# Sigmoid attention and a skip mixture of experts: scores and values as four 64x64 float32 products side by side

## The chip, the cores and the metric

The kernel runs on one core of a Trainium2 chip. The time is the device time of one execution in microseconds (us); the time of a kernel is the median of its runs.

## The reference

First an attention over q, k, v of shape (batch 8, heads 12, sequence 448, head size 64), in which a sigmoid takes the place of the softmax, so no sum over keys is needed:

```python
scores = scale * np.matmul(q, k.transpose(0, 1, 3, 2)) - np.log(S)
attn = 1.0 / (1.0 + np.exp(-scores))
out = np.matmul(attn, v)
```

The heads of a token are joined to a row of 768 numbers, 3584 rows in all. Then a layer of 8 experts with a skip:

```python
do_compute = x @ w_skip > 0          # the other rows pass through
e_idx = argmax(x @ w_gate)           # one expert for each row
y = x + gate_w * (relu(x @ w1[e_idx]) @ w2[e_idx])
```

w1 is 768 x 1024 and w2 1024 x 768 for each expert. All is float32.

## The kernel before, in words

**Attention** is a loop over 48 steps, one for each batch `b` and pair of heads `hp`. The order of all instructions in it is written out by hand, so each engine works them off in the order of the program. A step does the following.

- `load` (L176) brings in k and q of the pair two steps ahead, each in four DMAs of 32 partitions from SyncE's (SP's) queue, and v in one DMA of 112 partitions. The 32-row pieces are laid so that a transpose of 32x32 blocks on VectorE (DVE) is enough to turn k and q: afterwards the 64 numbers of a head lie on 64 partitions, one head of the pair on the upper half of the partitions and the other on the lower.
- `prep` (L200) turns k and q with that transpose and splits each into a high part in the type float32r and the rest (on DVE, and for q on GpSimd, POOL).
- `scores` (L219) multiplies on TensorE (PE): for each of four chunks of 112 keys the three products high x high, high x rest and rest x high, for two heads side by side in the upper and the lower rows of the array. A product streams 448 columns (queries).
- `weigh` (L237) runs the sigmoid over a chunk of both heads on ScalarE (ACT), from PSUM to SBUF.
- `values` (L242) multiplies a chunk's weights by v in float32, two heads side by side in the left and the right columns of the array, each over 112 rows (keys), and sums four chunks in one PSUM tile `pa`. It works on the step before: while step n's scores are made, the values of step n-1 are summed. At the end of a step DVE copies `pa` into `xts`, the transposed rows of the batch.

Chunks go in pairs: scores of two chunks, sigmoid of both, values of two chunks of the step before. PSUM holds three tiles of one bank for transposes (`ps_t`), two of two banks for scores (`ps_s`) and one of one bank for values (`ps_a`).

**Beside attention**, in the steps of batch b the rows of batch b-1 are finished. After step hp 0 the `logits` of gate and skip are made (PE), after hp 1 `route` turns them and picks the expert (PE, DVE), in hp 2 `gates` and `route_count` give each token a place in its expert's list and POOL scatters the records. In hp 1 to 4 `rows` turns one quarter of the batch's rows back (three transposes for each half, on PE), ACT and DVE copy them out and ACT's queue writes them. A quarter holds every fourth token (`col`, L253). In step 3 a fill of the expert lists goes out on SP's queue. From step 35 (`W0`) on, the first expert's weights are loaded in 28 pieces on SP's queue and split by DVE and POOL (`wsplit`).

**The experts** follow: two blocks of the first expert, during whose products a plan of the other blocks is worked out, and then a loop over 128-row blocks, whose kinds (full, last of an expert, half, few rows) depend on the counts. Some of its small kinds multiply in plain float32 with two or four products side by side in columns of the array (L1271 and L1204).

Of the kernel before, what the change touches and what calls it, by code (L numbers as in the profile page):

```python
# [20 lines left out]
P = 128  # L21
# [3 lines left out]
def kernel(  # L25
# [18 lines left out]
    BT = 32  # L44
    NJ = S // BT
# [38 lines left out]
    nc.scalar.dma_start(wcat[:, :, 0:NE], w_gate.rearrange("(k p) e -> p k e", p=P))  # L84
    with nc.allow_non_contiguous_dma(reason="one small vector"):
        nc.scalar.dma_start(
            wcat[:, :, NE : NE + 1], w_skip.rearrange("(k p o) -> p k o", p=P, o=1)
        )
# [13 lines left out]
    nc.gpsimd.iota(tok_i, pattern=[[1, NC]], base=0, channel_multiplier=NC)  # L102
# [45 lines left out]
        tc.tile_pool(name="ps_t", bufs=3, space=bass.MemoryType.PSUM)  # L148
# [23 lines left out]

    warm = const.tile([P, 1], F32, name="warm")
    nc.scalar.activation(warm, bias, AF.Sigmoid)

    def load(b, hp, q_eng=nc.sync):  # L176

        t = []  # L180
        n = (NJ - 1) * D + BT
        for nm, src, eng in (("k", k, nc.sync), ("q", q, q_eng)):
            x = io.tile([P, NJ * D], F32, tag=nm, name=f"{nm}_{b}_{hp}", bufs=2)
            for h in range(2):
                for i in range(ND):
                    p = h * D + i * BT
                    eng.dma_start(
                        x[p : p + BT, :n],
                        src[b, 2 * hp + h].rearrange("(r j) d -> r (j d)", j=NJ)[:, i * BT : i * BT + n],
                    )  # L190
            t.append(x)
        x = io.tile([CP, 2, NC, D], F32, tag="v", name=f"v_{b}_{hp}", bufs=3)
        nc.sync.dma_start(
            x.rearrange("p h c d -> p h (c d)"),
            v[b, 2 * hp : 2 * hp + 2].rearrange("h (p c) d -> p h (c d)", c=NC),
        )
        t.append(x)
        return t

    def prep(b, hp, kt, qt, first=False):  # L200

        out = []
        xs = wk.tile([P, 2, S], F32, tag="b0", name=f"x_{b}_{hp}")
        for nm, t, low in (("k", kt, nc.vector), ("q", qt, nc.gpsimd)):
            x = xs[:, len(out)]
            nc.vector.transpose(  # L206
                x.rearrange("p (r j) -> p j r", j=NJ),
                t.rearrange("p (j d) -> p j d", d=D)[:, :, :BT],
            )
            hl = wk.tile([P, 2, S], F32R, tag=nm + nm, name=f"{nm}{nm}_{b}_{hp}")  # L210
            if first:
                nc.scalar.activation(hl[:, 0], x, AF.Copy)  # L212
            else:
                nc.vector.tensor_copy(hl[:, 0], x)  # L214
            (nc.vector if first else low).tensor_tensor(hl[:, 1], x, hl[:, 0], op=ALU.subtract)  # L215
            out.append(hl)
        return out

    def scores(b, hp, cs, kk, qq):  # L219
        sc = {  # L220
            c: ps_s.tile([P, 2, 512], F32, tag="s", name=f"s_{b}_{hp}_{c}") for c in cs
        }
        for c in cs:

            for n, (a, w) in enumerate(((0, 0), (0, 1), (1, 0))):
                for j in range(2):
                    r = slice(j * D, (j + 1) * D)
                    nc.tensor.matmul(  # L228
                        sc[c][:CP, j, :S],
                        kk[r, a, c::NC],  # L230
                        qq[r, w, :],
                        start=(n == 0),
                        stop=(n == 2),
                    )
        return [sc[c] for c in cs]
# [1148 lines left out]
```

## Time and profile before

| | |
|---|---|
| median of 3 runs | 665.95 us (665.94 to 670.04) |
| profiled execution | 661.53 us |
| its span, first to last instruction | 659.8 us |
| mean granted clock of TensorE | 0.975 |
| busy PE / PE weight loads / DVE / ACT / POOL | 610.8 / 407.0 / 384.7 / 285.6 / 232.0 us |
| moved by DMA | 119.78 MB, mean 182 GB/s |

The profile is one execution. PE is TensorE's products, PEld its weight loads, which may overlap products, DVE VectorE, ACT ScalarE, POOL GpSimd, SP SyncE; an engine's name with a q is its queue of DMA issues. A group line gives line of the kernel, engine, operation, what is written and read, partitions x elements, the count after an x, then busy us, mean ns of one, and the idle time of the engine before them with what ended it. A float32 product of PE stands as two records. A timeline line begins with start and length in us; neighbouring instructions of one kind are merged, and the ends of products are modelled, so the lines of PE overlap a little: what counts is the distance from start to start. A line of the windows gives a stretch, its length, and for each engine busy us and instructions, then PE's granted clock, the DMA engines' busy share and GB/s. A line of the chain with a start and a length gives the time a group held the chain of work that ended last.

### The profile page before, as it was taken

The numbers are of one execution on the slowest core, as the hardware profiler recorded it, in microseconds if no ns is written. First come the engines' busy times: TensorE is split into PE (matmuls) and PEld (weight loads), VectorE is DVE, ScalarE is ACT, GpSimd is POOL, SyncE is SP. The second block draws the span as 40 slices with busy tenths as digits, with TensorE's granted clock in tenths as the row PEclk, the third lists the DMA queues.
The fourth block names the chain that finished last, engine by engine and source line by source line (L and its number), as shares of the span: only waits on it lengthen the run. The fifth ranks groups of instructions, "written<-read, shape, count | busy, mean of one in ns | idle before, by whom it ended". The sixth has DMA issues, their size and how long they took to land.

```text
span 659.8 us, 13758 instructions
## 1 busy us (share of the span) xinstructions
PE 610.8 (93%) x3843; PEld 407.0 (62%) x3844; DVE 384.7 (58%) x839; ACT 285.6 (43%) x463; POOL 232.0 (35%) x328
## 2 busy tenths in 40 slices
PE   5999999999999999998998999979799999999592
PEld 4555655656556555554454488968576768678382
DVE  4645766757667558588778466135733343437941
ACT  3654555555555546554454432226423212236430
POOL 1112411311313213156546632223822433437740
PEclk7999999999999999999999999998899999999797
DMA  9686665575775566696896413480484857869100
GB/s 187 174 252 170 177 182 167 181 208 148 207 209 171 152 187 187 193 247 191 242 231 201 143 43 99 116 323 3 136 292 154 309 193 243 289 231 338 41 20 25
DMA packets 62322, 119.78 MB, mean 182 GB/s; under 512 B 14036, under 2 KB 28132, under 8 KB 62272
## 3 DMA queue, kind: packets, MB, share of 16 engines
q1 hardware_dynamic: 52112, 99.01, 50.4%
q10 hardware_dynamic: 6128, 11.50, 5.8%
q0 software_dynamic: 4032, 8.65, 4.1%
q8 instruction: 25, 0.41, 0.3%
q14 instruction: 25, 0.20, 0.1%
HBM read 111.07 MB, written 17.86 MB: 195 GB/s over the span
## 4 chain that ended last, share of the span: by engine, by line
PE 75%; issue 7%; DMA 7%; DVE 4%; POOL 3%; ACT 1%; SPq 1%; ACTq 0%; POOLq 0%; DVEq 0%
PE pa L244 19%; PE s L228 18%; PE ph L509 9%; PE py L536 8%; PE px L283 4%; PE b_ph L509 3%; PE b_py L536 3%; DMA k<-in_k_dram 2%; PE ph L1271 2%; DMA q<-in_q_dram 2%; PE py L1271 2%; PE pxt L485 2%; PE pl L265 1%; PE ph L1204 1%; DMA lst<-fill 1%
## 5 line engine op out<-in xcount | busy, mean ns | idle before, releaser
L238 ACT ACTIVATE at<-s,bias 112x896 f32<-112x896 f32 x192 | 183.2, 1004 | 133.3 <-PE s L228 130.5
L228 PE MATMUL s<-qq,kk 64*112 64x448 f32 x1152 | 157.8, 405 | 11.5 <-ACT qq L212 5.1
L244 PE MATMUL pa<-at,v 112*64 112x448 f32 x752 | 165.6, 554 | 3.1 <-DVE xt L664 2.0
L228 PEld LDWEIGHTS s<-qq,kk 64*112 64x112 f32 x1152 | 127.2, 281 | 54.4 <-ACT at L238 23.6
L215 POOL TENSOR_TENSOR qq<-x,qq 128x448 fp32r<-128x448 f32 x47 | 53.8, 1144 | 220.9 <-DVE qq L214 159.4
L244 PEld LDWEIGHTS pa<-at,v 112*64 112x64 f32 x752 | 44.6, 135 | 60.3 <-issue 52.6
L206 DVE STREAM_TRANSPOSE x<-k 128x448 f32<-128x448 f32 x48 | 46.1, 960 | 16.9 <-DMA k<-in_k_dram 16.2
L283 PEld LDWEIGHTS px<-ident,xt 128*112 128x112 f32 x192 | 25.2, 188 | 40.2 <-issue 39.5
L664 DVE COPY xt<-pa 128x448 f32<-128x448 f32 x47 | 29.1, 620 | 35.4 <-PE pa L244 35.4
L292 DVE COPY xr<-px 112x384 f32<-112x384 f32 x28 | 15.6, 556 | 56.0 <-PE px L283 56.0
L206 DVE STREAM_TRANSPOSE x<-q 128x448 f32<-128x448 f32 x48 | 46.1, 961 | 2.3 <-DMA q<-in_q_dram 2.2
L414 POOL DMA_INDIRECT lst<-rec,idx x32 | 32.3, 1009 | 26.3 <-DVE xr L292 16.1
L283 PE MATMUL px<-ident,xt 128*112 128x128 f32 x192 | 36.4, 302 | 0.5 <-ACT xr L290 0.5
L518 ACT ACTIVATE hs<-ph 128x512 f32<-128x512 f32 x16 | 9.6, 600 | 62.6 <-PE ph L509 62.6
L479 POOL TENSOR_TENSOR wl<-wr,wh 128x384 fp32r<-128x384 f32 (+1 forms) x28 | 32.4, 1182 | 11.0 <-DVE wh L478 10.3
L509 PE MATMUL ph<-wh,xh 128*128 128x512 f32 x96 | 29.5, 409 | 5.0 <-issue 4.6
L536 PE MATMUL py<-wh,hh 128*128 128x384 f32 x128 | 33.8, 345 | 0.0
L536 PE MATMUL py<-wh,hl 128*128 128x384 f32 x128 | 32.7, 336 | 1.0 <-DVE hl L529 1.0
L529 DVE TENSOR_TENSOR hl<-pht,hh 128x512 fp32r<-128x512 f32 x16 | 11.0, 690 | 38.3 <-ACT hh L528 36.3
L215 DVE TENSOR_TENSOR kk<-x,kk 128x448 fp32r<-128x448 f32 x48 | 32.0, 666 | 1.6
L536 PE MATMUL py<-wl,hh 128*128 128x384 f32 x128 | 32.6, 335 | 0.0
L509 PE MATMUL ph<-wl,xh 128*128 128x512 f32 x96 | 30.4, 408 | 0.0
(276 smaller groups left out, 841.5 us busy)
## 6 DMA issues: line engine op xcount, KB each, us to landing
raw<-in_moe_w_dram SPq DMA_DIRECT2D x84, 256.0 KB
raw<-in_moe_w_dram SPq DMA_DIRECT2D x56, 384.0 KB
k<-in_k_dram SPq DMA_DIRECT2D x192, 108.0 KB
q<-in_q_dram SPq DMA_DIRECT2D x188, 108.0 KB
v<-in_v_dram SPq DMA_DIRECT2D x48, 224.0 KB
out_dram<-xr ACTq DMA_DIRECT2D x32, 336.0 KB
wr<-in_moe_w_dram SPq DMA_DIRECT2D x12, 256.0 KB
wr<-in_moe_w_dram SPq DMA_DIRECT2D x16, 192.0 KB
```

The costliest lines, as they stand in the source:

```text
L206: nc.vector.transpose(x.rearrange("p (r j) -> p j r", j=NJ), t.rearrange("p (j d) -> p j d", d=D)[:, :, :BT],)
L215: (nc.vector if first else low).tensor_tensor(hl[:, 1], x, hl[:, 0], op=ALU.subtract)
L228: nc.tensor.matmul(sc[c][:CP, j, :S], kk[r, a, c::NC], qq[r, w, :], start=(n == 0), stop=(n == 2),)
L238: nc.scalar.activation(at[c], sc[:CP, :, :S], AF.Sigmoid, bias=bias[:CP], scale=SCALE)
L244: nc.tensor.matmul(pa[j * D : (j + 1) * D, :S], vt[:, j, c, :], at[c][:, j, :], start=(c == 0), stop=(c == NC - 1),)
L283: nc.tensor.transpose(px[:CP, j * P : (j + 1) * P], xt[:, 3 * h + j, col(c)], ident,)
L414: put = nc.gpsimd.indirect_dma_start(out=lst[:, :], out_offset=bass.IndirectOffsetOnAxis(ap=idx[:, c : c + 1], axis=0), in_=rec[:, c, :], ...
L479: nc.gpsimd.tensor_tensor(lo, r, hi, op=ALU.subtract)
L509: nc.tensor.matmul(ph[h], a[:, j * P : (j + 1) * P], w[j][h], start=(n == 0), stop=(n == len(t) - 1),)
L536: nc.tensor.matmul(py[:, o, :H2], a[h][:, js], w[j][:, o * H2 : (o + 1) * H2], start=(j == 0 and n == 0), stop=(j == NK2 - 1 and n == 2),)
L664: nc.vector.tensor_copy(xts[prev[0]][:, prev[1], :], pa[:, :S])
L1271: nc.tensor.matmul(dst[g * MD : (g + 1) * MD, :n], a, w, start=(j == 0), stop=(j == most - 1), tile_position=(0, g * MD),)
```

## The change

- **Scores** are one float32 product for each head and chunk, without split. The 448 keys are taken as seven groups of 64 (every seventh key). A chunk `c` below 3 holds two of the groups (c and 4 + c); for each of two heads and two key groups there is one 64x64 product of 448 columns, the heads in the upper and lower rows of the array, the key groups in its left and right columns. Chunk 3 holds the seventh group (3): its two column halves take half of the queries each, 224 columns.
- **Values** use the same four parts: rows by key group, columns by head. The two row halves sum into two banks of `pa`, and DVE adds these: a copy of the first bank and an addition of the second (`add_values`).
- The values come **two chunks behind** the scores, in one line that runs across the steps, instead of a step behind.
- k and q are **loaded for two steps** by the same four DMAs of 32 partitions each, now with two runs in a row; v for two steps by two DMAs of 64 partitions with four of seven key groups each. Two buffers of each. The first step's k and q are loaded alone, q from ACT's queue ahead of the gate weights, which came first before.
- One chunk gives the place for the other work: after the scores of chunk 2, `rows` turns both halves at once, and logits and their turning stand there too (in the steps of hp 0 and 1), ahead of the values of that place. Row quarters hold 112 neighbouring tokens.
- PSUM: two tiles for transposes, two for scores of two banks, one for values of two banks. Some tiles of the experts' first blocks move to other buffers.

```diff
     ps_t = ctx.enter_context(
-        tc.tile_pool(name="ps_t", bufs=3, space=bass.MemoryType.PSUM)
+        tc.tile_pool(name="ps_t", bufs=2, space=bass.MemoryType.PSUM)
     )
...
+    def load_kq(b, hp, n, k_eng=nc.sync, q_eng=nc.sync, part=None, t=None):
+        if t is None:
+            t = [
+                wk.tile([P, n, NJ * D], F32, tag=nm, name=f"{nm}_{b}_{hp}", bufs=2) for nm in "kq"
+            ]
+        m = (NJ - 1) * D + BT
+        gs = slice(0, n) if part is None else slice(part, part + 1)
+        for x, src, eng in zip(t, (k, q), (k_eng, q_eng)):
             for h in range(2):
                 for i in range(ND):
                     p = h * D + i * BT
+                    a = src[b, 2 * hp : 2 * (hp + n)].rearrange(
+                        "(g h) (r j) d -> h r g (j d)", h=2, j=NJ
                     )
+                    eng.dma_start(x[p : p + BT, gs, :m], a[h, :, gs, i * BT : i * BT + m])
         return t
+    def load_v(b, hp, n):
+        x = io.tile([P, 2 * n, NV, D], F32, tag="v", name=f"v_{b}_{hp}", bufs=2)
+        a = v[b, 2 * hp : 2 * (hp + n)]
+        for m in range(2):
+            nc.sync.dma_start(
+                x[m * D : (m + 1) * D].rearrange("p h c d -> p h (c d)"),
+                a.rearrange("h (p c) d -> p h (c d)", c=NR7)[:, :, 3 * m * D : (3 * m + NV) * D],
+            )
+        return x
...
+    def scores(b, hp, c, xs):
+        sc = ps_s.tile([P, 2, 512], F32, tag="s", name=f"s_{b}_{hp}_{c}")
+        for m in range(2):
+            first, qs = (4 * m + c, slice(0, S)) if c < 3 else (3, slice(m * HQ, (m + 1) * HQ))
+            for j in range(2):
+                r = slice(j * D, (j + 1) * D)
+                nc.tensor.matmul(
+                    sc[m * D : (m + 1) * D, j, : qs.stop - qs.start],
+                    xs[r, 0, first::NR7],
+                    xs[r, 1, qs],
+                    start=True,
+                    stop=True,
+                )
+        return sc
...
+    def values(pa, c, vt, at):
+        for r in range(2):
+            rs = slice(r * D, (r + 1) * D)
+            qs = slice(0, S) if c < 3 else slice(r * HQ, (r + 1) * HQ)
+            for j in range(2):
+                nc.tensor.matmul(
+                    pa[j * D : (j + 1) * D, r, qs],
+                    vt[rs, j, r + c if c < 3 else 3 * (1 - r), :],
+                    at[rs, j, : qs.stop - qs.start],
+                    start=(c == 0),
+                    stop=(c == 3),
+                )
+    def add_values(b, hp, pa):
+        nc.vector.tensor_copy(xts[b][:, hp, :], pa[:, 0, :S])
+        nc.vector.tensor_tensor(xts[b][:, hp, :], xts[b][:, hp, :], pa[:, 1, :S], op=ALU.add)
...
+        if n % 2 and n + 3 < N:
+            kq[(n + 3) // 2] = load_kq(*steps[n + 3], 2)
...
+        for c in range(4):
+            at = wk.tile([P, 2, S], F32, tag="A", name=f"at_{b}_{hp}_{c}", bufs=5)
+            sc = scores(b, hp, c, xs)
+            weigh(c, sc, at)
+            if c == 0 and nxt:
+                xs_next = prep(*nxt, part(n + 1)[0])
+            if c == 2:
+                if hp == 0 and b > 0:
+                    pl = ps_t.tile([P, 512], F32, tag="t", name=f"pl_{pb}")
+                    logits(pl, range(NK1), xts[pb], 2)
+                if hp == 1 and b > 0:
+                    lg = turn_logits(pb, lts[pb])
+                rc = hp - (1 if b == B - 1 else 2)
+                if 0 <= rc < NC and b > 0:
+                    xr = new_xr(pb, rc)
+                    for h in range(2):
+                        rows(pb, rc, h, xts[pb], xr)
+            if len(line) == 2:
+                next_values()
+            line.append((b, hp, c, vt, at))
+            if c == 1:
+                if nxt:
+                    prep(*nxt, part(n + 1)[1], xs_next)
+                if n % 2 == 0 and n + 2 < N:
+                    vs[n // 2 + 1] = load_v(*steps[n + 2], 2)
...
```

`next_values` takes the oldest chunk of `line`, calls `values` for it and, after chunk 3, `add_values`; `prep` is one transpose for k (chunk 0) and one for q (chunk 1).

More of the change, by code (lines that the diff above doesn't have):

```diff
@@ L44 @@
     BT = 32
+    NR7 = S // D
+    NV = (NR7 + 1) // 2
     NJ = S // BT
@@ L83 @@
     nc.vector.memset(wcat, 0.0)
[L84 to L88, printed above, removed]
     ones = const.tile([CP, P], BF16, name="ones")
@@ L197, in load @@
[L197 to L217, printed above, removed]
@@ new lines, in prep @@
+    def prep(b, hp, t, xs=None):
+        n = 0 if xs is None else 1
+        if xs is None:
+            xs = wk.tile([P, 2, S], F32, tag="b0", name=f"x_{b}_{hp}")
+        nc.vector.transpose(
+            xs[:, n].rearrange("p (r j) -> p j r", j=NJ),
+            t.rearrange("p (j d) -> p j d", d=D)[:, :, :BT],
+        )
+        return xs
+    def scores(b, hp, c, xs):
[12 more added lines that the diff above has]
+        return sc
@@ L578, with part @@
     order.__enter__()
-    ld = {n: load(*steps[n], nc.scalar if n == 0 else nc.sync) for n in range(2)}
+    kq = {0: load_kq(0, 0, 2, nc.sync, nc.scalar, 0)}
+    load_kq(0, 0, 2, part=1, t=kq[0])
+    nc.scalar.dma_start(wcat[:, :, 0:NE], w_gate.rearrange("(k p) e -> p k e", p=P))
+    with nc.allow_non_contiguous_dma(reason="one small vector"):
+        nc.scalar.dma_start(
+            wcat[:, :, NE : NE + 1], w_skip.rearrange("(k p o) -> p k o", p=P, o=1)
+        )
+    warm = const.tile([P, 1], F32, name="warm")
+    nc.scalar.activation(warm, bias, AF.Sigmoid)
+    vs = {0: load_v(0, 0, 2)}
+    kq[1] = load_kq(*steps[2], 2)
+    def part(n):
+        return [t[:, n % 2] for t in kq[n // 2]]
     idle = ps_s.tile([P, 2, 512], F32, tag="s", name="idle")
@@ L585, in keep_busy, with next_values @@
             nc.tensor.matmul(idle[:, 0, :P], ident, ident, start=True, stop=True)
-    keep_busy(5)
-    pr = {0: prep(*steps[0], ld[0][0], ld[0][1], True)}
-    pr[1] = prep(*steps[1], ld[1][0], ld[1][1])
-    keep_busy(5)
-    prev = None
+    keep_busy(10)
+    xs = prep(*steps[0], part(0)[0])
+    xs = prep(*steps[0], part(0)[1], xs)
     xts, lts, rts = {}, {}, {}
     wrs = []
-    xr = None
+    line = []
+    pa = None
+    def next_values():
+        nonlocal pa
+        b, hp, c, vt, at = line.pop(0)
+        if c == 0:
+            pa = ps_a.tile([P, 2, 512], F32, tag="a", name=f"pa_{b}_{hp}")
+        values(pa, c, vt, at)
+        if c == 3:
+            add_values(b, hp, pa)
     for n, (b, hp) in enumerate(steps):
@@ L667 @@
         wrs = wrs_next
-        prev = (b, hp, ld.pop(n)[2], at)
-        if b > 0 and hp == 0:
-            pl = ps_t.tile([P, 512], F32, tag="t", name=f"pl_{pb}")
-            logits(pl, range(NK1), xts[pb], 2)
-            lts[pb] = keep_logits(pb, pl)
-        if b > 0 and hp == 1:
-            rts[pb] = route(pb, lts[pb])
+        xs = xs_next
     lb = B - 1
@@ L718 @@
     logits(pl, range(NK1 - 1), xt, 4)
-    pa = ps_a.tile([P, 512], F32, tag="a", name="pa_last")
-    for c in range(NC):
-        values(pa, c, prev[2], prev[3])
-    nc.vector.tensor_copy(xt[:, NPAIR - 1, :], pa[:, :S])
+    for _ in range(2):
+        next_values()
+    px = ps_s.tile([P, 2, 512], F32, tag="s", name="b0_px")
     for h in range(2):
-        px = ps_t.tile([P, 512], F32, tag="t", name=f"b0_px{h}")
-        turn_x(x0[0], h, px)
-        split_x(h, px, xh0, xl0)
+        turn_x(x0[0], h, px[:, h])
+        split_x(h, px[:, h], xh0, xl0)
     logits(pl, [NK1 - 1], xt, 4)
@@ L1015 @@
         gemm2(j, hh0, hl0, py)
-    pxt = [
-        ps_a.tile([P, 512], F32, tag="a", name="pxt0"),
-        ps_t.tile([P, 512], F32, tag="t", name="pxt1"),
-    ]
+    pxt2 = ps_a.tile([P, 2, 512], F32, tag="a", name="pxt")
+    pxt = [pxt2[:, h, :] for h in range(2)]
     for h in range(2):
```

127 lines of the change are left out of this document (36 added, 91 removed).

## The prediction, made before the changed kernel ran

> **What bounds the kernel now.** I read the page's parts 1 to 4 first, then its groups, then the timeline of TensorE alone (PE), because the question is how long one attention step occupies it.
>
> ```profile
> span 659.8 us, 13758 instructions
> PE 610.8 (93%) x3843; PEld 407.0 (62%) x3844; DVE 384.7 (58%) x839; ACT 285.6 (43%) x463; POOL 232.0 (35%) x328
> PE 75%; issue 7%; DMA 7%; DVE 4%; POOL 3%; ACT 1%; SPq 1%; ACTq 0%; POOLq 0%; DVEq 0%
> ...
> L238 ACT ACTIVATE at<-s,bias 112x896 f32<-112x896 f32 x192 | 183.2, 1004 | 133.3 <-PE s L228 130.5
> L228 PE MATMUL s<-qq,kk 64*112 64x448 f32 x1152 | 157.8, 405 | 11.5 <-ACT qq L212 5.1
> L244 PE MATMUL pa<-at,v 112*64 112x448 f32 x752 | 165.6, 554 | 3.1 <-DVE xt L664 2.0
> ```
>
> PE holds 75% of the chain that ended last, and scores (L228) and values (L244) are its two costliest groups. ACT, which turns scores into weights (L238), waited 130.5 us for scores, so it is not the limit. A step that carries only attention, and the start of a batch's extra work, look like this:
>
> ```profile
> 272.12 1.61 PE L228 MATMUL s<-qq,kk 64*112 64x448 f32 x12
> 273.65 1.72 PE L244 MATMUL pa<-at,v 112*64 112x448 f32 x8
> 275.31 1.60 PE L228 MATMUL s<-qq,kk 64*112 64x448 f32 x12
> ...
> 238.19 1.60 PE L228 MATMUL s<-qq,kk 64*112 64x448 f32 x12
> ...
> 282.97 1.60 PE L228 MATMUL s<-qq,kk 64*112 64x448 f32 x12
> ```
>
> From 272.12 to 275.31 passes half a step: two score chunks in 1.53 and two value chunks in 1.66, 3.19 in all, so **6.37 us a step**. The last two rows follow the logits of consecutive batches, so a batch of six steps takes 44.78. Less 6 x 6.37, **6.56 us** are left for the batch's other PE work (logits, row turning, counting). PE has no gaps here: attention is bound by PE.
>
> I cut the span at four marks:
>
> ```profile
> 50.02 0.57 PE L228 MATMUL s<-qq,kk 64*112 64x448 f32 x2 [1.28 <-DVE qq L214]
> 268.94 1.60 PE L228 MATMUL s<-qq,kk 64*112 64x448 f32 x12
> 374.77 1.20 PE L265 MATMUL pl_last<-xt,wcat 128*32 128x448 f32 x16
> ```
>
> Steps 0 to 5 end at 50.0; steps 6 to 34 take 218.9; steps 35 to 47, beside which the first expert's weights are loaded, take 105.8; the experts take the last 285.0. By PE work alone the third stretch would take 13 x 6.37 + 2 x 6.56 = 95.9, so about 10 us of it are stalls.
>
> **The new step on PE.** Which width a product streams at is seen in the expert code, where float32 products already run side by side in column parts of the array:
>
> ```profile
> 478.25 5.31 PE py L1271 x32
> 532.62 2.73 PE ph L1204 x48
> ```
>
> L1271 has two products of 384 columns side by side, 8 groups: 5.31 / 8 = 0.664. L1204 has four of 256 columns, 6 groups: 2.73 / 6 = 0.455. Read as one line, these give 1.63 ns a column and 0.037 us a group; two or four at once seems to make no difference. A group of 448 columns is then 0.768 us, one of 224 columns 0.402.
>
> The change has, per step, three score groups of 448 columns and one of 224, and the same for values: 6 x 0.768 + 2 x 0.402 = **5.41 us a step**, 0.96 less than 6.37. Today's values take 4 x 0.83 and would take 2.71; scores go from 3.05 to 2.71. The lower bound has no cost per group: 7 x 448 x 1.63 ns = 5.11. The upper bound gives every group the start that today's value block pays when PE turns from scores to values, 1.66 - 2 x 0.73 = 0.20: 5.11 + 8 x 0.20 = 6.7. I take the line through the two rows, since they show products of the same type, run after run in one shape, as the new groups would be. The assumption is that the parts may lie side by side in rows and columns at once; no row of before shows that for float32. Rows side by side are seen for scores only:
>
> ```profile
> 308.55 0.28 PEld L228 LDWEIGHTS s<-qq,kk 64*112 64x112 f32 x2 [0.70 <-issue]
> 329.74 1.32 PEld L228 LDWEIGHTS s<-qq,kk 64*112 64x112 f32 x12 [0.70 <-ACT at L238]
> 60.21 0.20 PEld L244 LDWEIGHTS pa<-at,v 112*64 112x64 f32 x4 [0.21 <-issue]
> 60.21 1.72 PE L244 MATMUL pa<-at,v 112*64 112x448 f32 x8
> 60.64 0.14 PEld L244 LDWEIGHTS pa<-at,v 112*64 112x64 f32 x2 [0.23 <-issue]
> 61.02 0.14 PEld L244 LDWEIGHTS pa<-at,v 112*64 112x64 f32 x2 [0.23 <-issue]
> ```
>
> Twelve score weight loads fill 1.32 of the 1.53 us, about 0.1 each, one after another: today's scores go at the pace of their weight loads. In the new step a group has eight loads of 64 columns. At 0.1 each they would be 0.8 a group, as long as the group; but the value rows show four such loads in 0.20 and the rest inside the products, and 64 columns are fewer than 112. I cost them at nothing beyond the 0.037; uncovered, they are the slower rival below.
>
> The Trainium skill, "TensorE: Matmul & The Clock Gate", section "The mechanism" of Part 3, says that a weight load overlaps products in flight only where its row group differs; two of the four new parts always share one. By that rule the 0.14 us loads would lie bare twice a group. This trace disagrees: the value loads at 60.64 and 61.02 share all rows with the products that run from 60.21 on, and the block still takes 1.66.
>
> **What hangs on the step.** ACT has three sigmoid passes of 896 elements and one of 448: 3 x 1.00 + an estimated 0.5 (half of it) = 3.5 us, below 5.41; the products that need them are two chunks away, about 3 us after the pass begins, so they hide. DVE loses the float32r splits and gains a second pass on the values:
>
> ```profile
> L664 DVE COPY xt<-pa 128x448 f32<-128x448 f32 x47 | 29.1, 620 | 35.4 <-PE pa L244 35.4
> L215 DVE TENSOR_TENSOR kk<-x,kk 128x448 fp32r<-128x448 f32 x48 | 32.0, 666 | 1.6
> L206 DVE STREAM_TRANSPOSE x<-k 128x448 f32<-128x448 f32 x48 | 46.1, 960 | 16.9 <-DMA k<-in_k_dram 16.2
> L215 POOL TENSOR_TENSOR qq<-x,qq 128x448 fp32r<-128x448 f32 x47 | 53.8, 1144 | 220.9 <-DVE qq L214 159.4
> ...
> 40.64 1.72 PE L244 MATMUL pa<-at,v 112*64 112x448 f32 x8
> 42.41 0.62 DVE L664 COPY xt<-pa 128x448 f32<-128x448 f32 x1 [2.48 <-PE pa L244]
> ```
>
> Two turns, a copy and an add (sized like the subtraction, 0.67) are 0.96 x 2 + 0.62 + 0.67 = 3.2 us a step, beside PE. POOL loses 1.14. The added wait: there is one values accumulator, so the next step's first value group waits for copy and add. The value block begun at 40.64 gives way after 1.66, at 42.30, and its copy starts 0.1 later; with as much for the way back that is 0.1 + 0.62 + 0.67 + 0.1 = 1.49 us, and PE has only one score group (0.77) to do meanwhile, with everything behind it in PE's order held: **0.7 us** bare. In batches 1 to 7 the logits or row turning stand at that place (6.56 / 6 is about 1.1 a step) and hide it; in steps 1 to 5 and 47 nothing does: 6 x 0.7 = 4.2.
>
> **Loads.** The same bytes of k and q (8 x 108 KB a step), values 256 KB instead of 224, in issues for two steps.
>
> ```profile
> k<-in_k_dram SPq DMA_DIRECT2D x192, 108.0 KB
> v<-in_v_dram SPq DMA_DIRECT2D x48, 224.0 KB
> out_dram<-xr ACTq DMA_DIRECT2D x32, 336.0 KB
> wr<-in_moe_w_dram SPq DMA_DIRECT2D x12, 256.0 KB
> wr<-in_moe_w_dram SPq DMA_DIRECT2D x16, 192.0 KB
> ...
> core 0: us, PE busy (x) PEld busy (x) DVE busy (x) ACT busy (x) POOL busy (x), PEclk, DMA share, GB/s
> 232.00:277.00 45.00, 44.78 (x296) 26.23 (x296) 30.79 (x70) 25.30 (x30) 11.02 (x12) 1.00 0.64 184
> 277.00:290.00 13.00, 13.00 (x88) 6.75 (x88) 9.22 (x16) 7.51 (x9) 5.68 (x5) 1.00 0.92 245
> 290.00:330.00 40.00, 35.78 (x216) 19.37 (x214) 33.47 (x61) 18.54 (x22) 23.70 (x22) 1.00 0.77 222
> ```
>
> A batch moves 6 x 1120 + 4 x 336 KB = 8.26 MB. A new batch on PE is 6 x 5.41 + 6.56 = 39.0 us: 212 GB/s, against 245 / 0.92 = 266 at full engines. The loads of k and q come out of SP's queue as soon as the second turn of the step before frees the tile, more than two steps (over 12 us) ahead; a pair needs 2240 KB, 8.6 us at 266. So they hide. In steps 35 to 44 they don't: 5 x 1728 (k, q) + 4 x 512 (v) + 4800 (21 weight pieces) + 6 x 336 (rows out) = 17.5 thousand KB, 17.9 MB, 67 us at 266, against 10 x 5.41 + about 10.5 = 65 on PE. There **DMA is late next**; with about 3 us of mismatch 70, and 19 for the last three steps: 89 instead of 105.8.
>
> **Start and end.**
>
> ```profile
> 6.85 0.95 DVE L206 STREAM_TRANSPOSE x<-k 128x448 f32<-128x448 f32 x1 [5.29 <-DMA k<-in_k_dram]
> 9.49 0.94 DVE L206 STREAM_TRANSPOSE x<-q 128x448 f32<-128x448 f32 x1 [0.43 <-DMA q<-in_q_dram]
> 11.09 5.20 PE L228 MATMUL s<-qq,kk 64*112 64x448 f32 x24 [5.13 <-ACT qq L212]
> ```
>
> Today q's issues stand behind the small gate loads and the table load on ACT. With those behind q, k and q should land together near 6.9; two turns later, at 8.8, scores start, without the 1.6 us of splitting: 2.3 earlier (bounds 0 and 4). Steps 0 to 5: 8.8 + 6 x 5.41 + 5 x 0.7 + about 1.7 (an estimate for the first values' load) = 46.5 instead of 50.0. At the end two value groups instead of four chunks remain: about 1.7 less, 283.3; the smaller transpose pool (two buffers for three) could take that back, 0 to +4.
>
> **Sum.** 46.5 + (29 x 5.41 + 5 x 6.56 + 0.7 = 190.4) + 89 + 283.3 = 609.2 us of span, against 659.8: -51. The profiled execution took 661.5 in all, the median of the runs is 665.95; I subtract from the median: **615 us**.
>
> **Rivals.** (1) Loads bind more: at the 222 GB/s that 290 to 330 reached while PE idled 4.2 of 40 us, the 17.9 MB take 81 instead of 70, and the pairs come late once or twice elsewhere: 11 + 4 more, 630. For it: stretch three stalls today; against: the batches need only 212. Chance 0.14. (2) Each group pays a start of 0.12 to 0.20, because the chunks alternate between two accumulators and wait on other engines: 6.07 to 6.7 a step, 0.66 to 1.29 more than forecast; the 35 steps up to the last stretch and the 3 after its loads feel it in full and the ten between mostly: 645 to 675. For it: that is what today's blocks pay; against: shape no longer changes between them. 0.09. (3) Slower: weight loads of the parts that share rows lie bare, 0.14 twice a group: 5.11 + 16 x 0.14 = 7.35 a step, 0.98 over today's, x 48 = 47 less 5 at start and end: 708. It decides from 0.08 bare per load on, where the step is 6.37 again. For it: scores today show loads in a line; against: the value block. 0.06. The cited rule of the Trainium skill speaks for this one. (4) The change does not do what it says: the parts run two and two, 10.8 a step, 4.4 x 48 more than today: about 870. 0.03.
>
> **How the numbers follow.** The forecast has 0.68. Its own range: no cost per group (0.3 a step, -9 in steps 6 to 34), loads without mismatch and start at its best (-3 each) give 600; the end's +4, the start's +2 and 0.04 more a group (0.3 a step, +9) give 630. To hold 8 in 10 the range takes rival 1 and the near end of rival 2: **600 to 643**. Within 1% (about what a measurement of this kernel can tell from no change) lies part of rival 2: 0.04. Slower by over 1% are rivals 3 and 4 and the far end of 2: 0.09. Faster 0.87.
>
> **What would show it.** Plain steps of 5.4 us from score group to score group, with groups 0.77 long; six waits of PE for the add, 0.7 each, in steps 1 to 5 and 47; a first score near 8.8; DMA share over 0.9 and waits for k in steps 35 to 44; an unchanged loop over experts. I am wrong if the groups take over 0.85, if DVE waits for k in the middle batches, or if the add takes over 1 us.

## The result, and the profile after

The changed kernel took **639.94 us** (median of 4 executions, 637.68 to 644.19) against 666.33 for the kernel before on the same chip: a ratio of 0.960, 95% interval 0.955 to 0.965. A second measurement beside other variants gave 641.84 (638.44 to 646.49), ratio 0.964 (0.957 to 0.972). The forecast was 615 with a range of 600 to 643: direction and range hold, but of the forecast gain only half came. The time lies 3 us inside the range, in the room that the range left for rivals; the forecast's own range, 600 to 630, was missed.

The page of the changed kernel's profiled execution (the one of 644.19 us), its engines and the groups of scores (L220) and values (L241):

```profile
PE 573.6 (90%) x4995; PEld 376.1 (59%) x4996; DVE 332.2 (52%) x744; ACT 276.1 (43%) x461; POOL 175.7 (28%) x281
...
L241 PE MATMUL pa<-at,v 64*64 64x448 f32 (+1 forms) x1536 | 170.4, 506 | 19.2 <-DVE xt L251 17.8
L220 PE MATMUL s<-x 64*64 64x448 f32 (+1 forms) x1536 | 170.1, 506 | 5.4 <-DVE x L205 4.7
```

TensorE is busy 37 us less. Waits for the addition of the two value banks (L251), 17.8 us, are new. Where the span went, by the marks of the prediction; in each profile step 6 and step 35 begin with the first scores line of that step (48.98 and 236.72 in the first profile, 49.26 and 237.36 in the second):

| stretch, us | before | forecast | after | second profile of after |
|---|---|---|---|---|
| steps 0 to 5 | 50.0 | 46.5 | 49.0 | 49.3 |
| steps 6 to 34 | 218.9 | 190.4 | 187.7 | 188.1 |
| steps 35 to 47, to the last logits | 105.8 | 89 | 104.7 | 106.9 |
| from there to the end | 285.0 | 283.3 | 296.4 | 287.3 |
| span | 659.8 | 609.2 | 637.8 | 631.6 |
| time less span | 1.7 | taken as unchanged | 6.4 | 7.3 |

The whole gain lies in steps 6 to 34. The last 13 steps, for which 17 us were forecast, gave nothing.

The timeline of TensorE in a step of the first batch (start, length, then what was done; a row ends with the idle time before it and its releaser):

```profile
30.34 0.96 PE L220 MATMUL s<-x 64*64 64x448 f32 x8
31.09 0.96 PE L241 MATMUL pa<-at,v 64*64 64x448 f32 x8
...
32.59 0.59 PE L241 MATMUL pa<-at,v 64*64 64x224 f32 x8
32.97 0.96 PE L220 MATMUL s<-x 64*64 64x448 f32 x8
34.66 0.98 PE L241 MATMUL pa<-at,v 64*64 64x448 f32 x8 [0.73 <-DVE xt L251]
...
91.01 1.34 PE L266 MATMUL pl<-xt,wcat 128*32 128x448 f32 x16
129.76 1.34 PE L266 MATMUL pl<-xt,wcat 128*32 128x448 f32 x16
246.45 1.34 PE L266 MATMUL pl<-xt,wcat 128*32 128x448 f32 x16
300.85 1.34 PE L266 MATMUL pl<-xt,wcat 128*32 128x448 f32 x16
341.42 1.15 PE L266 MATMUL pl_last<-xt,wcat 128*32 128x448 f32 x16
```

A group of four products comes every 0.75 us at 448 columns and every 0.38 at 224 (forecast 0.768 and 0.402), so a step holds 5.25 us of attention. The row at 34.66 is the bare wait for copy and add. The logits rows lie one batch of six steps apart: 38.75 between the first two (all five early batches: 38.5 to 39.2, forecast 39.0), then **54.40 for steps 36 to 41** and 40.57 for steps 42 to 47.

What stands in the 54.40 is seen in five views of the same profile: TensorE, then VectorE ahead of the longest wait, then VectorE's waits from 246 to 341 us (total, times, longest), then three of the waits of SP's queue in the same stretch, then the issues of that queue.

```profile
257.85 1.77 PE L241 MATMUL pa<-at,v 64*64 64x448 f32 x8 [4.05 <-DVE xt L251]
292.54 1.77 PE L241 MATMUL pa<-at,v 64*64 64x448 f32 x8 [6.40 <-DVE xt L251]
...
288.04 0.43 DVE L482 CAST wh<-wr 128x512 fp32r<-128x512 f32 x1 [7.08 <-DMA wr<-in_moe_w_dram]
...
290.35 0.93 DVE L205 STREAM_TRANSPOSE x<-k 128x448 f32<-128x448 f32 x1
291.14 0.59 DVE L250 COPY xt<-pa 128x448 f32<-128x448 f32 x1
291.77 0.62 DVE L251 TENSOR_TENSOR xt<-xt,pa 128x448 f32<-128x448 f32 x1
...
DVE wh L482 <- DMA wr<-in_moe_w_dram: 18.8, 9, 7.1
...
SPq L473 <- DMA out_dram<-xr: 9.4, 2, 7.2
SPq L186 <- DMA out_dram<-xr: 9.2, 2, 5.7
SPq L194 <- DMA out_dram<-xr: 8.6, 2, 5.4
...
240.46 9.19 SPq L186 DMA_DIRECT2D q<-in_q_dram  x4
250.73 2.52 SPq L473 DMA_DIRECT2D wr<-in_moe_w_dram  x5
```

VectorE stands 7.08 us at a cast (L482) whose weight piece has not landed. The turn of k, the copy and the add of the next step are behind it in VectorE's order; the add ends at 292.4, and TensorE goes on at 292.54. Before, all such waits for pieces were 0.7 us in sum. In a step SP asks for the pieces behind k and q, and the four q issues that begin at 240.46 and stand ahead of pieces took 9.19 us. SP's waits name what held the queue longest: from 246 to 341 us issues of pieces (L473), of k and q (L186) and of v (L194) stood 27.2 us until a row store (`out_dram<-xr`, rows written out from ScalarE's queue) had landed. Such holds alone do no harm: the four q issues at 226.47 took 9.15 us, and TensorE lost nothing by it. No run took the row stores away, so how much of the loss they make is open.

### The profile page after: what moved, and what is told of

Same layout as the page of the kernel before. It is cut to its first block, busy times and chain, and to the rows that moved or that the text cites. A ratio compares the mean times of both kernels' runs of the same rounds, so it can differ in the third digit from the quotient of the medians.

```text
span 637.8 us, 15511 instructions
## 1 busy us (share of the span) xinstructions
PE 573.6 (90%) x4995; PEld 376.1 (59%) x4996; DVE 332.2 (52%) x744; ACT 276.1 (43%) x461; POOL 175.7 (28%) x281
## 5 line engine op out<-in xcount | busy, mean ns | idle before, releaser
L233 ACT ACTIVATE at<-s,bias 128x896 f32<-128x896 f32 x192 | 175.2, 914 | 134.7 <-PE s L220 127.0
L241 PE MATMUL pa<-at,v 64*64 64x448 f32 (+1 forms) x1536 | 170.4, 506 | 19.2 <-DVE xt L251 17.8
L220 PE MATMUL s<-x 64*64 64x448 f32 (+1 forms) x1536 | 170.1, 506 | 5.4 <-DVE x L205 4.7
L220 PEld LDWEIGHTS s<-x 64*64 64x64 f32 x1536 | 82.8, 191 | 63.0 <-issue 39.1
L241 PEld LDWEIGHTS pa<-at,v 64*64 64x64 f32 x1536 | 59.9, 136 | 71.5 <-issue 56.0
L205 DVE STREAM_TRANSPOSE x<-k 128x448 f32<-128x448 f32 x48 | 45.9, 957 | 24.5 <-DMA k<-in_k_dram 13.6
L284 PEld LDWEIGHTS px<-ident,xt 128*112 128x112 f32 x192 | 20.1, 133 | 20.2 <-issue 17.5
L251 DVE TENSOR_TENSOR xt<-xt,pa 128x448 f32<-128x448 f32 x48 | 29.8, 620 | 1.6
L499 DVE TENSOR_TENSOR xl<-pxt,xh 128x384 fp32r<-128x384 f32 x30 | 16.4, 554 | 26.5 <-ACT xh L495 26.1
L284 PE MATMUL px<-ident,xt 128*112 128x128 f32 x192 | 28.0, 280 | 1.7 <-ACT xr L291 1.7
L540 PEld LDWEIGHTS py<-wh,hl 128*128 128x128 f32 x128 | 24.2, 197 | 8.5 <-DVE hl L533 8.5
```

Of the source, the lines that this page charges most:

```text
L205: nc.vector.transpose(xs[:, n].rearrange("p (r j) -> p j r", j=NJ), t.rearrange("p (j d) -> p j d", d=D)[:, :, :BT],)
L220: nc.tensor.matmul(sc[m * D : (m + 1) * D, j, : qs.stop - qs.start], xs[r, 0, first::NR7], xs[r, 1, qs], start=True, stop=True,)
L233: nc.scalar.activation(at[:, :, :n], sc[:, :, :n], AF.Sigmoid, bias=bias, scale=SCALE)
L241: nc.tensor.matmul(pa[j * D : (j + 1) * D, r, qs], vt[rs, j, r + c if c < 3 else 3 * (1 - r), :], at[rs, j, : qs.stop - qs.start], start=( ...
L251: nc.vector.tensor_tensor(xts[b][:, hp, :], xts[b][:, hp, :], pa[:, 1, :S], op=ALU.add)
L284: nc.tensor.transpose(px[:CP, j * P : (j + 1) * P], xt[:, 3 * h + j, col(c)], ident,)
```

## The experiments

The question of most of them is why steps 35 to 47 gained nothing. The reading above, theory A of the first one: the first expert's weight pieces come late, VectorE stands at their casts, and TensorE waits for the add behind them. Each expectation says what its own letters mean. "Steps 36 to 41" and "42 to 47" are the distances between logits rows; the changed kernel has 54.4 and 40.6 there (54.3 and 42.8 in its second profile).

**No weight transfers.** Each cast reads one small tile filled once, in place of a piece that was loaded.

```diff
-        nc.sync.dma_start(r, src[ds(ev, 1), ...])
+        r = wz[:, :n]
```

> The changed kernel without the 28 transfers of the first expert's weights: their casts and subtractions stay, but read one constant tile, so the first expert's result is left out. Theory A (in steps 35 to 47 the casts on DVE stand in its order ahead of the turns and the add, and wait for weight pieces that land late; PE then waits for the add): the four long PE waits of 4.1, 1.2, 6.4 and 2.1 us go, steps 36 to 41 take 39 to 40 us like the batches before, not 54.4, and the time falls by 14 to 18 us to about 624. Theory B (the stretch is set by something on PE or ACT, such as a lower granted clock): steps 36 to 41 stay above 48 us, time 636 to 642.

621.4 us, span 616.9 (one execution). Steps 36 to 41 took 39.9, steps 42 to 47 37.8; no wait of TensorE over 1 us is left in them. Logits rows and TensorE, VectorE and DMA from 246 to 300 us (the columns are length, busy us and instructions of the five engines, granted clock, DMA share, GB/s):

```profile
250.84 1.34 PE L266 MATMUL pl<-xt,wcat 128*32 128x448 f32 x16
290.71 1.34 PE L266 MATMUL pl<-xt,wcat 128*32 128x448 f32 x16
...
246.00:300.00 54.00, 52.37 (x597) 28.20 (x594) 39.05 (x77) 31.39 (x39) 25.62 (x25) 1.00 0.87 201
```

So all that the last stretch lost hangs on these 6.3 MB of transfers: 77.7 us against 95.0 for the twelve steps.

**The pieces asked for ahead of k and q** in SP's queue, the rest unaltered.

```diff
+        if 0 <= n - W0 < len(how_many):
+            for _ in range(how_many[n - W0]):
+                wrs_next.append(wload(units.pop(0), ev0))
         if n % 2 and n + 3 < N:
             kq[(n + 3) // 2] = load_kq(*steps[n + 3], 2)
...
-        if 0 <= n - W0 < len(how_many):
-            for _ in range(how_many[n - W0]):
-                wrs_next.append(wload(units.pop(0), ev0))
```

> The changed kernel with one move: in each step the weight pieces are issued on SP's queue ahead of the k and q loads of that step, not behind them. The bytes are the same. Theory A (the pieces are late because they are issued late, behind 1.7 MB of k and q that have over two steps of time): DVE's waits for pieces, 18.8 us, fall below 6 and the time falls by 8 to 13 us, to 627 to 632. Theory B (the DMA engines are full in this stretch, whatever the order): the waits move to k and q, the time stays within 3 us of 640.

629.36 us (627.88 to 634.44), ratio to the kernel before 0.941 (0.937 to 0.946), as theory A said. Steps 36 to 41 took 48.1, steps 42 to 47 40.5. From 246 to 341 us VectorE now waits 3.8 us for pieces and 9.5 for k and q.

**The pieces from ScalarE's queue.**

```diff
-        nc.sync.dma_start(
+        nc.scalar.dma_start(
```

> The changed kernel with the 28 weight pieces issued on ACT's queue, not SP's; the bytes are the same. Theory A (the pieces are late because SP's queue works off k, q and v first): DVE's waits for pieces fall below 4 us, time down by 10 to 15 us to 625 to 630, if ACT's own stream of 0.33 us issues does not stall. Theory B (the DMA engines are full): within 3 us of 640, with waits for k and q in their place. Theory C (ACT is held at its issues while the queue is full, as SP is): PE waits for ACT's sigmoid passes and the time rises by 5 us or more.

639.47 us (635.22 to 642.77), ratio 0.959 (0.953 to 0.964): no gain, as theory B said. Steps 36 to 41 took 51.8 and 42 to 47 38.8, but steps 30 to 35 grew to 42.6. VectorE's waits moved to q (18.4 us in the whole span, 5.1 in the changed kernel; for k 13.9 and 13.6). Another queue alone does not help.

**The changed kernel again**, beside three of the variants below.

> The changed kernel unaltered, as the measure for the three others and to see which part of its first profiled execution (span 637.8, of which 296.4 us after the last logits, against 285.0 before) belongs to the kernel. If the change made the experts longer by itself, the part after the last logits is again 294 to 298 us. If that was the scatter of one execution, it is 286 to 291, as in the three variants that were run so far. Steps 36 to 41 should again take 52 to 55 us in place of 39.

287.3 us after the last logits: the 296.4 belongs to the scatter between executions, and so does a 294.3 in the profile of the next variant; this one and nine of variants with the same choice of experts have 286.7 to 290.0. What makes the two long is open. What is left here, 2.2 over before, lies ahead of the loop over experts: the first product of its first block comes 49.9 us after the last logits in place of 47.4, and the loop takes 237.4 (before 237.7).

**The same 28 pieces, later**: 10 in place of 14 in steps 35 to 40.

```diff
-    how_many = (3, 2, 2, 2, 3, 2, 3, 2, 2, 2, 3, 2)
+    how_many = (1, 2, 1, 2, 1, 3, 2, 3, 3, 3, 4, 3)
```

> The same 28 weight pieces, but 10 of them in steps 35 to 40 (14 before) and 18 in steps 41 to 46 (14 before): fewer where k and q are still loaded, more where nothing else is. Theory A (what slows steps 36 to 41 is that k, q, v, out and weights together ask for all that the DMA engines move, some 233 GB/s at 0.90 share, while 300 to 340 us runs at 181): steps 36 to 41 fall from 54.4 to 42 to 47 us, steps 42 to 47 grow from 40.6 to 41 to 45, total 628 to 635. Theory B (a weight piece is late because SP's queue is held by the q loads ahead of it, whatever the number of pieces): the waits of the cast for its piece stay at 4 to 7 us each and the total at 636 to 642.

642.74 us (635.31 to 644.24). Steps 36 to 41 fell to 50.9 and steps 42 to 47 rose to 42.2; a cast still waits up to 7.9 us. Theory B's numbers came within 1 us, A's did not: with fewer pieces in the queue one is as late as before.

**Both: later, and ahead of k and q.**

> The late spread of the 28 weight pieces, and in each step the pieces asked for ahead of k and q. Theory A: with less asked for in steps 36 to 41 neither the pieces nor k and q come late, and the total is 622 to 630, near the 621.4 of the kernel without these transfers. Theory B (order alone decides): the same as with the order alone changed, 628 to 634.

629.73 us (626.94 to 633.36), ratio 0.944 (0.938 to 0.951): the edge of A's range, and as the order alone. Steps 36 to 41 took 42.2, steps 42 to 47 44.6. VectorE's waits from 246 to 341 us:

```profile
DVE x L205 <- DMA q<-in_q_dram: 9.5, 4, 3.7
DVE x L205 <- DMA k<-in_k_dram: 6.0, 2, 3.6
...
DVE wh L482 <- DMA wr<-in_moe_w_dram: 1.8, 3, 0.7
```

Of 18.8 us for pieces 1.8 are left, and 15.5 for k and q have come: something is still late when the order is good.

**The cast on GpSimd**, loads unaltered.

```diff
     def wsplit(r, hi, lo):
-        nc.vector.tensor_copy(hi, r)
+        nc.gpsimd.tensor_copy(hi, r)
```

> The cast of a weight piece moved from VectorE to GpSimd, which does the subtraction behind it anyway; order and number of the loads unaltered. Theory A (what TensorE loses in steps 36 to 47 is VectorE standing at a late piece, with the next step's turn, copy and add behind it in its order): the pieces come as late as before, but GpSimd stands in VectorE's place, the waits of TensorE for the add fall under 0.5 us, steps 36 to 41 take 39 to 43 us and the total is 622 to 630. Rival C (the bandwidth is short, and k and q come late once VectorE does not wait for the pieces): steps 36 to 41 take 46 us or more and the total is 631 to 640. Rival H (a cast on GpSimd is so slow that the 28 of them set the end of the stretch): steps 42 to 47 grow by over 4 us.

632.32 us (628.50 to 636.38, 6 executions), ratio 0.945 (0.941 to 0.949). GpSimd, then TensorE at the same time:

```profile
290.07 0.61 POOL L482 CAST wh<-wr 128x512 fp32r<-128x512 f32 x1 [7.57 <-DMA wr<-in_moe_w_dram]
...
290.61 1.04 PE L220 MATMUL s<-x 64*64 64x448 f32 x8 [1.86 <-DVE x L205]
```

The piece is as late (7.57 us) and GpSimd stands there in VectorE's place. Steps 36 to 41 take 42.4, as A said. What A did not say: TensorE's waits for the add do not all fall under 0.5 (the longest is 1.5), TensorE now waits for the turn of a late q (1.86), and steps 42 to 47 take 43.5, so the total lies 2 us above its range and in rival C's. What is left is C's kind: late loads of k and q.

**The first expert chosen a batch earlier and its pieces spread over 18 steps**, ahead of k and q.

```diff
-    W0 = N - 13
-    how_many = (3, 2, 2, 2, 3, 2, 3, 2, 2, 2, 3, 2)
+    W0 = N - 19
+    how_many = (1, 1, 2, 1, 2, 1, 2, 1, 2, 1, 2, 1, 2, 1, 2, 2, 2, 2)
...
-                if hp == 3 and b == B - 3:
+                if hp == 3 and b == B - 4:
```

> The version meant to beat both: the weight pieces asked for ahead of k and q, the first expert chosen one batch earlier (after step 27 instead of 33), and the 28 pieces spread over steps 29 to 46, one or two in each. Theory A (in steps 35 to 47 the bytes asked for exceed the some 240 GB/s that the DMA engines give, so a part of the loss is bandwidth and goes only by moving bytes to a stretch with room): steps 30 to 35 grow from 39 to 40 to 42, steps 36 to 41 take 40 to 43, steps 42 to 47 39 to 42, total 619 to 627. Rival C (the steps before have no room either: 217 GB/s at a DMA share of 0.90): what is gained behind is lost in steps 30 to 35, and the total stays at 627 to 633 as with the order alone changed.

632.80 us (632.09 to 634.04), ratio 0.945 (0.941 to 0.948). The window from 246 to 300 us:

```profile
246.00:300.00 54.00, 49.80 (x557) 26.20 (x552) 33.23 (x66) 29.74 (x37) 16.27 (x17) 1.00 0.99 247
```

Steps 30 to 35 grew to 42.8, steps 36 to 41 took 43.0, steps 42 to 47 39.7: each close to A's number, 125.4 in all against 125.8 in the variant "later and ahead". The DMA engines are full (0.99), and moving pieces forward costs there what it saves behind: rival C. The early batches of this execution took 39.7 to 40.0 against 38.5 to 39.6 there, so in the stretches a gain of up to 3 us could hide; the total shows none.

**k and q a step at a time**, four buffers of one step.

```diff
-        wk.tile([P, n, NJ * D], F32, tag=nm, ..., bufs=2) for nm in "kq"
+        wk.tile([P, n, NJ * D], F32, tag=nm, ..., bufs=4) for nm in "kq"
...
-        if n % 2 and n + 3 < N:
-            kq[(n + 3) // 2] = load_kq(*steps[n + 3], 2)
+        if n + 3 < N and n > 0:
+            kq[n + 3] = load_kq(*steps[n + 3], 1)
```

> k and q loaded one step at a time, into four buffers of one step in place of two of two; the same bytes and rows of the same length, twice as many DMAs of half the size. Theory A (the bytes in the stretch decide): steps 36 to 41 stay at 50 to 55 us and the total at 633 to 642. Rival D (loading two steps at once asks for 1.4 MB in one burst, and the weights queue behind it): without the burst steps 36 to 41 fall to 42 to 47 and the total to 627 to 633.

644.02 us (640.03 to 648.37), ratio 0.963 (0.956 to 0.971). Steps 36 to 41 took 52.9; the burst of two steps (eight DMAs of 216 KB, 1.77 MB and not 1.4) is not the cause. The early batches became longer (40.2 to 44.5 in four of five), with waits of TensorE for v.

**Values with 128 rows in place of two times 64**: the scores stay as four 64x64 products, a full chunk's values become two products side by side, for one half of the queries and then the other, with the same columns to stream.

```diff
-            rs = slice(r * D, (r + 1) * D)
-            qs = slice(0, S) if c < 3 else slice(r * HQ, (r + 1) * HQ)
+            rs = slice(0, P) if c < 3 else slice(r * D, (r + 1) * D)
+            qs = slice(r * HQ, (r + 1) * HQ) if c < 3 else slice(0, HQ)
```

> The changed kernel with values of chunks 0 to 2 as products over all 128 rows, two heads side by side in columns, once for each half of the queries (224 columns each); chunk 3 stays as four 64x64 products. Each half of the queries has its own bank, so the add on DVE goes and the wait for the accumulator falls from 0.7 to 0.1 us where it is bare. The streamed columns are the same. Theory A (what the four 64x64 parts bring for values is that the shape of the array's parts does not change between scores and values; each change costs the 0.16 to 0.2 us that the value block of the kernel before pays): six starts a step, +0.6 to +1.2 us a step, time 665 to 690. Theory B (a change of shape costs nothing here): plain steps stay at 5.27, about 5 us of waits go, time 633 to 637.

657.54 us (656.08 to 661.05), ratio 0.985 (0.979 to 0.991).

```profile
61.97 0.56 PE L241 MATMUL pa<-at,v 64*64 64x224 f32 x8
62.35 0.93 PE L220 MATMUL s<-x 64*64 64x448 f32 x8
...
66.21 1.04 PE L220 MATMUL s<-x 64*64 64x448 f32 x8
67.18 0.98 PE L241 MATMUL pa<-at,v 128*64 128x224 f32 x8
68.09 1.04 PE L220 MATMUL s<-x 64*64 64x448 f32 x8
...
99.37 1.34 PE L267 MATMUL pl<-xt,wcat 128*32 128x448 f32 x16
143.19 1.34 PE L267 MATMUL pl<-xt,wcat 128*32 128x448 f32 x16
```

Where the shape stays (61.97 to 62.35, 224 columns) the pace is 0.38 as before; from 66.21 to 67.18 and on to 68.09, where it changes, the same columns take 0.97 and 0.91 in place of 0.75. A batch takes 43.82 in place of 38.75: 0.85 us a step, some 0.14 for each of six changes. Theory A's size per step, 0.6 to 1.2, is met; its total was too high, since the last twelve steps did not grow: 94.2 us against 95.0. The Trainium skill, "TensorEngine Tiling (Array Packing)", section "Key Properties", says that changing the tiling mode drains TensorE. The rows agree, and here is its price.

**Values one chunk behind** in place of two.

```diff
-            if len(line) == 2:
+            if len(line) == 1:
                 next_values()
```

> The values product one chunk behind its scores in place of two. From the changed kernel's rows a chunk's weights are ready about 2.1 us after its scores begin (PE at 30.34, ScalarE at 31.43 for 1.01). One behind, 2.25 us pass between scores and values of the middle chunks, but only 1.9 where the half chunk lies between. Theory A: a wait of 0.2 to 0.3 twice a step, batches of 40 to 42 us, total 645 to 660. Rival F (the wait for copy and add lies at the same place and covers these): batches stay at 38.5 to 39.5 and the total at 636 to 646.

684.90 us (682.82 to 686.55), ratio 1.023 (1.019 to 1.027): slower than the kernel before, and outside both expectations. TensorE, its waits for the add in the whole span (total, times, longest), and the logits rows:

```profile
106.69 0.93 PE L220 MATMUL s<-x 64*64 64x448 f32 x8
108.37 0.98 PE L241 MATMUL pa<-at,v 64*64 64x448 f32 x8 [0.74 <-DVE xt L251]
110.03 0.65 PE L306 MATMUL pg<-ident,lt 128*112 128x128 f32 x4
...
PE pa L241 <- DVE xt L251: 45.2, 40, 5.4
...
102.36 1.34 PE L266 MATMUL pl<-xt,wcat 128*32 128x448 f32 x16
147.92 1.34 PE L266 MATMUL pl<-xt,wcat 128*32 128x448 f32 x16
```

The expectation looked at ScalarE and missed the place. Two behind, the first values product of a step follows chunk 2, where logits and row turning stand and cover copy and add. One behind, it follows chunk 1 (108.37), and the other work comes after it (110.03): the wait is bare in most steps, 45.2 us in 40 waits where the changed kernel has 17.8 in 13. The total grew by 45.0; a batch takes 45.56 (102.36 to 147.92) in place of 38.75.

**No copy of the first bank.**

```diff
-        nc.vector.tensor_copy(xts[b][:, hp, :], pa[:, 0, :S])
-        nc.vector.tensor_tensor(xts[b][:, hp, :], xts[b][:, hp, :], pa[:, 1, :S], op=ALU.add)
+        nc.vector.tensor_tensor(xts[b][:, hp, :], bias.to_broadcast([P, S]), pa[:, 1, :S], op=ALU.add)
```

> One half of the sum over the row halves is left out: the copy of the first bank goes and the add reads the second bank alone, so VectorE holds the bank pair for one operation of 0.62 us in place of two; x, and with it the choice of experts, is another, so only the batches before the experts are compared. Theory A (TensorE sets the batches, and their 0.7 us waits at the first values product of a step are the copy and add): the wait falls to 0.1 or less in five steps of six, batches of 35.3 to 36.5 us in place of 38.5 to 39. Rival G (the k and q loads set the batches, at their DMA share of 0.90): the wait for the add is replaced by one for the turn of k or q, and the batches stay at 38 to 39.

The program took 885.75 us with its other choice of experts, so only the batches count. The waits for the add went, in steps 1 to 5 too:

```profile
32.92 0.93 PE L220 MATMUL s<-x 64*64 64x448 f32 x8
33.84 0.98 PE L241 MATMUL pa<-at,v 64*64 64x448 f32 x8
...
91.55 1.34 PE L265 MATMUL pl<-xt,wcat 128*32 128x448 f32 x16
131.29 1.34 PE L265 MATMUL pl<-xt,wcat 128*32 128x448 f32 x16
```

From the score group of chunk 2 to the first values product of the step pass 0.92 us, where the changed kernel has 1.69 (32.97 to 34.66). But the batches did not get shorter: 39.7. Theory A's number was built on a wrong premise of the expectation: from step 6 on these waits are covered anyway, so there was nothing to take from a batch. G's number nearly came, without its cause: no wait for k or q shows in the early batches, and TensorE is at work. That a batch is 1 us longer than 38.75 is no cost of this edit: the run without weight transfers has 39.2 to 39.9 in the same batches. For the prediction this settles that copy and add cost some 0.8 us in each of the first five steps without cover, and nothing in the covered ones.

## Why the prediction was right, and where not

The mechanism of the gain was right; one term of the sum, the last stretch, was not, and the range held only because it had room for that.

- **The step.** Right: 5.25 us of groups a step against 5.41 forecast. Four 64x64 float32 products side by side run at the pace read from two products of other shapes, and the line's cost per group was nearer zero. Steps 6 to 34 came 2.7 us below the forecast.
- **Weight loads at nothing.** Right: eight loads of 64 columns a group leave the group at 0.75 us. Rival 3 (bare loads of parts that share rows, 708) is out, and with it what the cited rule of the Trainium skill would give for this kernel; the starts of rival 2 appear only where the shape alternates (the 128-row values), and rival 4 is out too.
- **The wait for the add.** Right in place, and nearly in size: 0.69 to 0.81 us of idle time in steps 1 to 5 (34.66 comes 1.69 after the group before it, in place of 0.75: 0.94 a step against 0.7) and 1.10 in step 47. The cover by logits and row turning was right; with the values one chunk behind it is gone, and the time grew by 45 us, 27 of them in more idle time at this wait.
- **Start.** First scores at 9.64 us against 8.8 (before 11.09). The first three score groups then took 1.52 us each, at a granted clock of 0.50 from 9.6 to 14.2 us, where the sum has 0.77. Steps 0 to 5 came 2.5 us late.
- **Loads beside the last stretch: the step that failed.** It said "with about 3 us of mismatch 70, and 19 for the last three steps: 89", and 104.7 to 106.9 were measured. Bytes over bandwidth was the right view and "DMA is late next" the right name; wrong was the price of lateness. Steps 35 to 44 took 81.6 us (236.72 to 318.33) for the 70, the last three 23.1 for the 19. The sign that it named, waits for k, did not come either: from 246 to 341 us VectorE waits for no k or q, but 18.8 us for pieces. Three things were missing. The bytes: in steps 35 to 44 the changed kernel asks for 23 pieces, five loads of v and seven row stores, where the sum has 21, four and six; that is 19.2 MB in place of 17.9, 4.7 us at its 266 GB/s. The order: a late piece does not only delay its own cast, it stops an engine that TensorE needs every step, and TensorE then runs on at half its clock. Asking for the pieces first (88.6 us for steps 36 to 47, 86.8 with the later spread) or casting on GpSimd (85.8) took back a third to a half of what the transfers cost (95.0 with them, 77.7 without). And the bandwidth, which is argued: the rest stayed in the four variants that gained, with the DMA engines busy 0.94 to 0.99 from 246 to 300 us, and the best such window moved 247 GB/s, so 266 in the mean was too much. The 266 came from a row of the kernel before; the early batches of the changed one moved 217 at a share of 0.90, or 241 at full. Rival 1 was the nearest: its 81 us for steps 35 to 44 came, and its 15 us are a little under the 15.7 to 17.9 that the stretch lost, but not by bandwidth alone.
- **The end.** The loop over experts is unchanged (237.4 us, before 237.7), as forecast. Ahead of the loop, the second profile lies 4.0 us over the forecast, at the edge of the smaller pool's bound of 0 to +4. That the pool itself costs this was not tried. The first profile lies 13.1 over, by scatter.
- **Outside the span.** The sum took what lies around the span as unchanged. It was 1.65 to 1.75 us in all 32 executions of the kernel before that ran beside the variants, and 5.6 to 8.3 in 8 of the changed one: some 5 us of the gain that no term foresaw. The variants spread from 1.7 (values with 128 rows) to 8.1 (the later pieces). The traces show what stands there, transfers of the kind "instruction" (last section); why the changed kernel has them at its end is open.

Summed up for the second profile (638.92 us, 23.9 over the forecast): 17.9 for the last stretch, 2.8 for the start, 4.0 for the end and 5.6 outside the span, less 2.3 in the middle steps and the 4.4 by which the median that the forecast subtracts from lies over the profiled execution: 23.6.

The version that beats both kernels is the changed one with its pieces asked for first: ratio 0.941 (0.937 to 0.946), apart from the changed kernel's interval (0.955 to 0.965). "Later and ahead", the cast on GpSimd and the early choice lie within its uncertainty.

## What to carry to other kernels

When a change makes one engine faster, sum up the bytes of each stretch at the new pace, and then follow a late transfer through the in-order engine that takes it: what stands behind that instruction is what the lateness costs. Look at the DMA queue the same way: an issue that waits for another transfer to land holds all requests behind it. A wait that is free has a cover with a place; moving the work by one position can lay it bare in most steps. Keep neighbouring products of TensorE in one shape, even where another shape would stream the same columns.

## What the runs showed of the hardware beyond that

**A wait costs twice.** After the long waits TensorE's granted clock is lower. Two windows of the changed kernel, the first behind the wait of 6.40 us, the second 1.3 us behind the start that ended one of 2.06:

```profile
292.50:296.00 3.50, 3.46 (x24) 1.72 (x28) 2.54 (x5) 0.64 (x1) 2.28 (x3) 0.50 1.04 227
326.20:329.20 3.00, 3.00 (x22) 1.35 (x19) 1.97 (x3) 0.64 (x1) 2.60 (x3) 0.51 1.01 326
...
294.80 1.75 PE L241 MATMUL pa<-at,v 64*64 64x448 f32 x8
296.30 1.75 PE L220 MATMUL s<-x 64*64 64x448 f32 x8
324.86 0.98 PE L241 MATMUL pa<-at,v 64*64 64x448 f32 x8 [2.06 <-DVE xt L251]
```

At a clock of 0.50 a group takes 1.50 us (294.80 to 296.30) in place of 0.75. From 292.54 to 298.86 lie five groups that need 3.4: 2.9 us lost beside the 6.40. With 1.5 behind the wait at 257.85 and the waits themselves (4.05, 1.16, 6.40) that makes 16.0, near the 15.7 by which steps 36 to 41 exceed a batch of 38.75. Where the waits are gone (the run without weight transfers), the clock is 1.00 from 246 to 341 us. In all thirteen profiles of the changed kernel and its variants, from 45 us to the last logits, each of the 22 waits of 2.06 us and more is followed by a fall to 0.50; of the 35 waits of 1.0 to 2.0 us two are. The Trainium skill, "TensorE: Matmul & The Clock Gate", section "What's actually happening", has the half clock follow an idle window of about 3.4 us. The half clock agrees; but waits from 2.06 us on were enough here, and the waits of 0.7 in steps 1 to 5 were not.

**The DMA engines' busy share is not the bytes.** Before, 184 GB/s went with a share of 0.64; in the early batches of the changed kernel, 217 with 0.90 (first line); in its steps 36 to 41, 232 with 0.89 (second):

```profile
53.00:246.00 193.00, 191.52 (x2180) 103.80 (x2172) 118.58 (x245) 116.92 (x145) 20.86 (x28) 1.00 0.90 217
246.45:300.85 54.40, 42.79 (x440) 22.06 (x436) 31.68 (x62) 23.69 (x30) 21.66 (x20) 0.87 0.89 232
```

In the early batches TensorE waited 1.5 us in 193, in the other stretch 11.6 in 54.40, at the same share. The share alone does not tell whether transfers come in time.

**Transfers behind the last instruction.** What the DMA queues moved from the end of the span on, first in the changed kernel (queue and kind, packets, MB, share), then in the kernel before:

```profile
q14 instruction: 3, 0.02, 0.1%
...
DMA packets 0, 0.00 MB, mean 0 GB/s; under 512 B 0, under 2 KB 0, under 8 KB 0
```

In the changed kernel the last of the three ends 6.7 us behind the last instruction, and 6.4 us lie outside the span. The fourteen profiles fall into two groups: four (the kernel before, values with 128 rows, the cast on GpSimd, no copy) show no transfer there and have 1.7 to 1.8 us outside the span; ten show such transfers, all of the kind "instruction", and have 4.2 to 7.8. That they hold the end up is argued from this; no run changed them.
